# Program order from the first attention pair on, and weight steps moved from beside attention into the block products

## The chip, the cores and the metric

The kernel runs on one core of one Trainium2 chip, as one program. The metric is device time in microseconds (us) per execution. The kernel before took 1133.33 us, the median of three runs (1131.05 to 1134.03).

## The reference, cut to what matters

Chunked attention with a few memory keys feeds two dense layers in turn. Everything is fp32.

```python
batch, n_heads, seq, head_dim = (4, 8, 768, 64); n_mem = 8
chunk, left_ctx, right_ctx = (32, 16, 8)
for c in range(seq // chunk):                # each chunk of 32 queries sees at most 56 keys and 8 memory keys
    scores = scale * (q_c @ k_full.T)
    out[:, :, chunk_c] = softmax(scores) @ v_full
x = out.transpose(0, 2, 1, 3).reshape(3072, 512)
h = x @ w_in                                 # 512 -> 2048
x = np.maximum(0.01 * h, h) @ w_out          # 2048 -> 512
a, b = x @ w_a, x @ w_b                      # 512 -> 1536, twice
y = (a * b) @ w_out2                         # 1536 -> 512
```

## The kernel before

**Numbers.** TensorE works on fp32r operands. Each fp32 operand is split into a high part (a copy by ScalarE, ACT) and a low part (a subtraction by VectorE, DVE), and each product is three matmuls: low by high, high by low, high by high.

**Attention** is cut into 24 units of 128 tokens. A unit has 32 score matmuls (`a_scores`), a softmax on DVE and ACT, a transpose and 32 matmuls with the values. Units 0 to 7 are worked before or beside block 0 of the first dense layer; the other 16 go in pairs, and the list `STARTS` (18, 24, 29, ... 55, 60) says beside which item a pair begins.

**First dense layer, blocks 0 to 3.** The 3072 tokens are six blocks of 512. Blocks 0 to 3 are worked in items numbered 16 x block + f, with f one of 16 slices of the hidden width. One item has `mm1_pe` (12 matmuls into a PSUM tile `h`, of which there are two), `mm1_act` (ACT: the leaky relu, which releases `h`, and the copy `gh`; then DVE: the low part `gl`), and, two items late, `mm2` (12 matmuls into four PSUM tiles `a` that collect over all f). Block 0 has three more items (16 to 18 in its own counting), in which the second half of its tokens catches up on the first slices. When a block is done, ACT copies the four `a` tiles to SBUF tiles `x` (three buffers, tag `z`), and SyncE (SP) stores them to HBM. The next block's `mm2` needs the four `a` tiles free.

**Block products, blocks 4 and 5.** These two blocks are multiplied as 2 x 2 blocks with seven products in place of eight (the loop `for p in range(NF1 // 2)`, eight pairs of f slices). A pair has seven products of six matmuls (`prod`, into tiles A, B and C) and two `mm2`. The partial sums go through ACT snapshots `u` and DVE sums `s`; `relu` makes `g`, `gh` and `gl` of them, or, for block 5, a tile `g5` that is kept in SBUF. `late` is the last sum of a pair; its relu is written in the next pair. `s_sums` and `s_parts` make the summed weights (`zs`, `sc`, `sw`) for the pair to come.

**Weight steps.** The weights of the last two layers are split and combined ahead of time by the generator `prep_steps`, in 18 sets. `step()` takes two of its parts; four such steps (72 in all) make a set: two steps with a bias on ACT and a join on DVE for one 512 KB load `raw` each (tile `pz`), one step with copies on ACT (`pwa`) and four combinations and the low parts on DVE (`ps`, `pwa`), and one step with a copy on ACT and a low part on DVE (`pwb`) and the stores to HBM. In an item with n steps one part goes ahead of `mm1_pe`, and the other 2n - 1 stand between `mm1_pe` and `mm1_act`. The function `steps_at` says how many steps an item has.

**Order.** The framework's planner lists the instructions of each engine by its own estimate of when they are ready. `InOrder` replaces that by the order of the program for an engine while `on` is true. PE, DVE, ACT and SP are so from the start to the end of `first_items`; all four are then left to the planner for the rest of block 0, and PE, DVE and ACT are in program order again from item 16 (`if bi == 1 and f == 0`). In program order all instructions carry the line of the helper, L46 or L49. SBUF tiles of one tag take turns over a few buffers, so a writer can wait for the last reader of an older tile; tag `t` (tiles `g`, `u`, `sc`) has four.

**Last layers.** From about 613 us on the last two layers run, with TensorE busy almost without a gap.

Of the kernel before, what the change touches and what calls it, by code (L numbers as in the profile page):

```python
# [24 lines left out]
NF1, NF2 = F1 // P, F2 // P  # L25
# [30 lines left out]
def kernel(  # L56
# [68 lines left out]
    class Weights:  # L125
# [58 lines left out]
        def step(self):  # L184
            if self.joined < self.loaded:
                self.join()
                self.bias(self.joined + 2)
                self.low(self.joined - 1)
            else:
                self.low(self.joined)  # L190
# [218 lines left out]
    def x_raw():  # L409
        for h, tag in enumerate(("xh", "xl")):  # L410
            xr[NL + h] = xp.tile([P, KC, TB], F32, tag=tag, name="xr")
        for k in x4d:
            sp.dma_start(out=xr[NL][:, :, k * UT:k * UT + UT], in_=x4d[k])
# [10 lines left out]
    def x_tiles(key):  # L424
        hi = xp.tile([P, KC, TB], F32R, tag="xh", name="xh")
        lo = xp.tile([P, KC, TB], F32R, tag="xl", name="xl")
        x1[key] = (hi, lo)
# [87 lines left out]
    def mm1_pe(bi, parts):  # L515
        ps = ps_h.tile([P, TB], F32, tag="h", name="h")
        for o, n, f in parts:
            proj(ps, wslot[f, 0], x1["x", bi], slice(o, o + n))
        c = slice(min(o for o, _, _ in parts), max(o + n for o, n, _ in parts))
        return ps, c  # L520

    def mm1_act(ps, c, low=True):
        g = tp.tile([P, TB], F32, tag="t", name="g")
        act.activation(g[:, c], ps[:, c], AF.Prelu, alpha=0.01)
        gh = tp.tile([P, TB], F32R, tag="gh", name="gh", bufs=3)
        gl = tp.tile([P, TB], F32R, tag="gl", name="gl", bufs=3)
        act.copy(gh[:, c], g[:, c])

        def rest():
            dve.tensor_tensor(  # L530
                out=gl[:, c], in0=g[:, c], in1=gh[:, c].bitcast(F32), op=ALU.subtract
            )
            return gh, gl

        return rest() if low else rest

    def mm1(bi, parts):
        return mm1_act(*mm1_pe(bi, parts))
# [54 lines left out]
    def at(bi, f, fn, *args):  # L593
        beside.setdefault((bi, f), []).append(lambda: fn(*args))
# [78 lines left out]
    def at_item(i, *args):  # L673
        at(*divmod(i, NF1), *args)
# [20 lines left out]
    STARTS = (18, 24, 29, 34, 40, 45, 50, 55, 60)  # L695
# [191 lines left out]
    def wo_load(upto):  # L887
        while wo_next[0] < upto:
            b, f = 1 + wo_next[0] // NF1, wo_next[0] % NF1
            if b == NB3:  # L890
                break
            t = wop.tile([P, 2, 512], F32R, tag="wo", name="w")
            nc.sync.dma_start(out=t.bitcast(F32), in_=wod[f])
            wslot[f, 1] = t
            wo_next[0] += 1
# [21 lines left out]
    def y_part(i):  # L917
        t = y_raw(Y[i]).rearrange(two)
        hi, lo = [y_home(i, l) for l in range(2)]
        ya[i] = hi, lo  # L920
        hi, lo = hi.rearrange(two), lo.rearrange(two)
        act.copy(hi, t)
        dve.tensor_tensor(out=lo, in0=t, in1=hi.bitcast(F32), op=ALU.subtract)
# [21 lines left out]
        y_sub(1, 1, 2)  # L945

    def s_begin():
        s_sums(0)
        s_parts(0, 0)
        s_parts(0, 1)  # L950

# [2 lines left out]
    def s_sums(p):  # L954
        zs = []
        for f in (2 * p, 2 * p + 1):
            w = wslot[f, 0]
            z = tp.tile([P, 512], F32, tag="z", name="zs", bufs=3)
            dve.tensor_tensor(out=z, in0=w[:, 0].bitcast(F32), in1=w[:, 1].bitcast(F32), op=ALU.add)
            zs += [z[:, 0:256], z[:, 256:512]]  # L960
        z11, z12, z21, z22 = zs
        t = [tp.tile([P, 2, 256], F32, tag="t", name="sc") for _ in range(2)]
        for o, x, y, op in (
            (t[0][:, 1], z21, z22, ALU.add),
            (t[0][:, 0], t[0][:, 1], z11, ALU.subtract),
            (t[1][:, 0], z11, z21, ALU.subtract),
            (t[1][:, 1], z12, t[0][:, 0], ALU.subtract),
        ):
            dve.tensor_tensor(out=o, in0=x, in1=y, op=op)
        sums_[p] = t  # L970

    def s_parts(p, h):
        t = sums_[p][h]
        w = xa.tile([P, 2, 2, 256], F32R, tag="sw", name="sw", bufs=3)
        act.copy(w[:, 0], t)
        dve.tensor_tensor(out=w[:, 1], in0=t, in1=w[:, 0].bitcast(F32), op=ALU.subtract)
        for k, n in enumerate(((2, 3), (4, 6))[h]):
            sw[p, n] = w[:, :, k]
# [14 lines left out]

    at_item(max(STARTS), y_begin)
    at_item(max(STARTS) + 1, y_subs)
    at_item(max(STARTS) + 2, s_begin)

    def steps_at(i):
        if i < STARTS[0]:
            return 3  # L1000
        s = [x for x in STARTS if x <= i][-1]
        return (2, 1, 0, 0, 3, 2)[i - s] if s < STARTS[-1] else 0

    late = None
    for bi, f, parts in items[LEAD:]:
        i = (bi - 1) * NF1 + f
        first = bi == 0
        if f == 0 and not first:
            if bi + 1 < NL:
                x_tiles(("x", bi + 1))  # L1010
            else:
                x_raw()
        if bi == 1 and f == 0:
            for e in (pe, dve, act):
                e.on, e.last = True, None
        if first:
            W1.load(2 * f + 14)
            W1.step()
            behind.append((bi, parts, mm1(bi, parts)))
            W1.step()  # L1020
        else:
            n = steps_at(bi * NF1 + f)
            if n:
                next(steps, None)
            ps = mm1_pe(bi, parts)
            if late:
                behind.append(late[:2] + (late[2](),))
            for k in range(n):
                next(steps, None)
                if k + 1 < n:  # L1030
                    next(steps, None)
            late = bi, parts, mm1_act(*ps, low=False)
        if len(behind) >= LAG + first:
            mm2(*behind.pop(0))
        for fn in beside.get((bi, f), []):
            fn()
        if not first:
            wo_load(i + 3)
        elif f >= NF1 - 1:
            wo_load(f - NF1 + 2)  # L1040
            prep_load(f - NF1 + 1)
            if f > NF1:
                step()
    behind.append(late[:2] + (late[2](),))


    def relu(src, kept=None):
        g = tp.tile([P, TB], F32, tag="t", name="g")
        act.activation(g, src, AF.Prelu, alpha=0.01)
        if kept is None:  # L1050
            gh = tp.tile([P, TB], F32R, tag="gh", name="gh", bufs=3)
            gl = tp.tile([P, TB], F32R, tag="gl", name="gl", bufs=3)
        else:
            w = wp.tile([P, 2, TB], F32R, tag=f"wi{kept}", name="g5")
            gh, gl = w[:, 0], w[:, 1]
        act.copy(gh, g)

        def low():
            dve.tensor_tensor(out=gl, in0=g, in1=gh.bitcast(F32), op=ALU.subtract)
            return gh, gl  # L1060

        return low
# [26 lines left out]
    kept, late = {}, None  # L1089
    for p in range(NF1 // 2):  # L1090
        f0, f1 = 2 * p, 2 * p + 1
        A = ps_h.tile([P, TB], F32, tag="h", name="A")
        prod(A, p, 0, 0, True)
        Bk = ps_s.tile([P, TB], F32, tag="s", name="B")
        if not p:
            pe.matmul(Bk, wslot[0, 0][:, 0, 0:P], ya[0][0][:, 0], start=True, stop=True)
        act.copy(Bk, A)
        if p:
            low12 = relu(late, f1 - 2)
        else:  # L1100
            y_part(2)
        next2(behind.pop(0))
        if p:
            kept[f0 - 2] = low12()
        prod(Bk, p, 1, 1, False)
        g11 = relu(Bk)()
        if p + 1 < NF1 // 2:
            s_sums(p + 1)
        prod(A, p, 2, 4, False)
        u2 = snapped(A)  # L1110
        if p == 0:
            y_part(6)
        C = ps_s.tile([P, TB], F32, tag="s", name="C")
        prod(C, p, 3, 3, True)
        if p + 1 < NF1 // 2:
            s_parts(p + 1, 0)
            s_parts(p + 1, 1)
        prod(A, p, 4, 5, False)
        u3 = snapped(A)
        s22 = summed(u3, C)  # L1120
        next2(part2(NL, f0, g11))
        kept[f1] = relu(s22, f0)()
        if p:
            step()
        prod(A, p, 5, 2, False)
        low21 = relu(A)
        prod(C, p, 6, 6, False)
        behind.append(part2(NL, f1, low21()))
        if p:
            step()  # L1130
        late = summed(u2, C)
    low12 = relu(late, f1)
    next2(part2(NL + 1, 0, kept[0]))
# [518 lines left out]
```

## Time and profile before

| | |
|---|---|
| median of three runs | 1133.33 us |
| the profiled execution's own time | 1134.86 us |
| its span, first to last instruction | 1133.1 us |
| TensorE (PE) busy | 1101.9 us, 97% |
| VectorE (DVE) busy | 777.3 us, 69% |
| ScalarE (ACT) busy | 527.2 us, 47% |
| mean granted TensorE clock | 0.993 of full speed |

All times are us from the start of the span unless marked ns. A row of a timeline is one instruction, or several alike (x and their count); the bracket at its end is how long the engine was idle before it, and what ended that. The clock is the share of full speed that was granted; the two levels are 1.2 and 2.4 GHz. Stages: attention and block 0 up to about 129 us, blocks 1 to 3 beside attention to about 437, block products to about 565, the rest of block 5 to about 613, last layers to the end.

### The profile page before, as it was taken

Reading aid. Unit: us, or ns where it says so; the run is one execution under the profiler, and the core shown is the slowest. Engines: PE = TensorE matmul, PEld = TensorE weight load, DVE = VectorE, ACT = ScalarE, POOL = GpSimd, SP = SyncE. Lnnn points to the kernel's source line nnn. Section 1 sums busy time; section 2 is a strip of 40 time slices with the busy share of each in tenths; the row PEclk is TensorE's granted clock in tenths of the full one; section 3 lists DMA queues with packets and bytes.
Section 4 is the critical chain, followed back from the end, with each engine's and each line's share of the span. In section 5 each row is a group of like instructions: output and inputs, shape, how many; then the busy total and the mean of one; then the engine's idle time right before and its main releaser. Section 6 shows DMA issues by size and latency. Waiting matters only on the chain.

```text
span 1133.1 us, 16325 instructions
## 1 busy us (share of the span) xinstructions
PE 1101.9 (97%) x6195; PEld 914.1 (81%) x6195; DVE 777.3 (69%) x1417; ACT 527.2 (47%) x893; POOL 7.4 (1%) x18
## 2 busy tenths in 40 slices
PE   7899889999999999999999999999999999999997
PEld 6788768878888887877788888888888888888886
DVE  6796378989898877667540645678745678745666
ACT  5887454555555545565531434243433233343232
POOL 2000000000000000000000000000000000000000
PEclk9999979999999999999999999999999999999999
DMA  9996898889988862433586857576867476767452
GB/s 318 381 353 229 280 326 322 288 309 319 353 330 311 312 244 94 148 139 121 195 315 233 288 164 225 159 231 187 272 216 252 143 242 191 232 179 242 144 188 75
DMA packets 99855, 270.63 MB, mean 239 GB/s; under 512 B 9665, under 2 KB 24129, under 8 KB 99009
## 3 DMA queue, kind: packets, MB, share of 16 engines
q1 hardware_dynamic: 98032, 267.88, 69.5%
q10 hardware_dynamic: 1744, 1.70, 0.5%
q8 instruction: 49, 0.80, 0.3%
q14 instruction: 30, 0.24, 0.1%
HBM read 215.02 MB, written 54.53 MB: 238 GB/s over the span
## 4 chain that ended last, share of the span: by engine, by line
PE 85%; DVE 8%; ACT 3%; DMA 2%; issue 1%; SPq 0%; DVEq 0%; ACTq 0%
PE ca L49 18%; PE a L49 16%; PE cc L49 9%; PE oa L49 8%; PE h L49 8%; PE cb L49 5%; PE oy L49 4%; PE A L49 2%; PE pv L49 2%; DVE pt L49 2%; PE oz L49 1%; PE s L49 1%; PE h L432 1%; PE C L49 1%; PE h L433 1%; PE a L556 1%
## 5 line engine op out<-in xcount | busy, mean ns | idle before, releaser
L49 PE MATMUL ca<-ch,wab 128*128 128x512 f32 x576 | 192.5, 390 | 0.0
L49 PE MATMUL a<-gh,w 128*128 128x512 f32 (+1 forms) x536 | 175.6, 390 | 6.7 <-ACT x L49 6.2
L49 PE MATMUL h<-xh,w 128*128 128x512 f32 (+1 forms) x407 | 133.1, 390 | 4.3 <-ACT g L49 3.6
L49 ACT CAST st<-gb 128x512 fp32r<-128x512 f32 x126 | 76.5, 621 | 124.6 <-DVE gb L49 124.0
L49 PEld LDWEIGHTS ca<-ch,wab 128*128 128x128 f32 x576 | 108.2, 188 | 23.2 <-ACT a L49 0.5
L49 PEld LDWEIGHTS a<-gh,w 128*128 128x128 f32 x536 | 101.2, 190 | 29.1 <-ACT x L49 8.2
L49 PE MATMUL ca<-cl,wab 128*128 128x512 f32 x288 | 112.3, 390 | 0.0
L49 PE MATMUL a<-gl,w 128*128 128x512 f32 (+1 forms) x268 | 104.6, 390 | 3.0 <-DVE gl L49 3.0
L49 PE MATMUL oa<-st,wt 128*128 128x512 f32 x420 | 104.3, 389 | 0.0
L49 PE MATMUL cc<-ch,wab 128*128 128x512 f32 x288 | 100.5, 390 | 0.0
L49 DVE TENSOR_TENSOR st<-gb,st 128x512 fp32r<-128x512 f32 x126 | 85.3, 689 | 15.0 <-ACT st L49 13.3
L49 PEld LDWEIGHTS h<-xh,w 128*128 128x128 f32 x407 | 76.5, 190 | 20.3 <-ACT g L49 3.9
L49 PEld LDWEIGHTS oa<-st,wt 128*128 128x128 f32 x420 | 78.9, 188 | 16.3
L49 ACT COPY u<-ca 128x512 f32<-128x512 f32 x72 | 42.2, 586 | 91.6 <-PE ca L49 91.4
L49 DVE STREAM_TRANSPOSE pt<-p 32x128 f32<-32x128 f32 x256 | 77.4, 302 | 3.3
L49 PE MATMUL h<-xl,w 128*128 128x512 f32 (+1 forms) x204 | 78.9, 387 | 0.3 <-DVE xl L49 0.3
L49 PEld LDWEIGHTS cc<-ch,wab 128*128 128x128 f32 x288 | 54.1, 188 | 11.3
L49 PEld LDWEIGHTS ca<-cl,wab 128*128 128x128 f32 x288 | 54.1, 188 | 11.1
L49 PEld LDWEIGHTS a<-gl,w 128*128 128x128 f32 x268 | 51.0, 190 | 14.5 <-DVE gl L49 4.6
L49 DVE TENSOR_TENSOR gl<-g,gh 128x512 fp32r<-128x512 f32 (+1 forms) x67 | 45.2, 676 | 19.6 <-ACT gh L49 19.1
L49 PE MATMUL cc<-cl,wab 128*128 128x512 f32 x144 | 56.1, 390 | 0.0
L49 PE MATMUL oy<-st,wt 128*128 128x512 f32 x216 | 53.8, 389 | 0.0
(186 smaller groups left out, 1906.2 us busy)
## 6 DMA issues: line engine op xcount, KB each, us to landing
wab<-wab SPq DMA_DIRECT2D x126, 512.0 KB, 4.4
w<-wod SPq DMA_DIRECT2D x80, 512.0 KB, 5.5
raw<-w SPq DMA_DIRECT2D x68, 512.0 KB, 7.0
wt<-wtd SPq DMA_DIRECT2D x63, 512.0 KB, 4.4
k<-kl SPq DMA_DIRECT2D x48, 256.0 KB, 5.5
v<-vl SPq DMA_DIRECT2D x48, 256.0 KB, 5.8
wab<-pwb SPq DMA_DIRECT2D x12, 768.0 KB, 3.3
wod<-w SPq DMA_DIRECT2D x16, 512.0 KB, 6.4
```

Of the source, the lines that this page charges most:

```text
L49: self.last = emit(*args, **kwargs).ins
L432: pe.matmul(ps, w[1], x[0], start=first, stop=False)
L433: pe.matmul(ps, w[0], x[1], start=False, stop=False)
L556: pe.matmul(ps, slot[:, 1, c], gh[:, t], start=f == 0 and o == 0, stop=False, **kw)
```

## The change

The program order begins at item 18, where the first pair of units starts, instead of item 16. Items 16 and 17 have one step instead of three, the items 33 and 49 (the second item of a block) one instead of three, and the two steps at the end of block 0 are gone. The parts of the weights that are summed for the first pair of the block products (`s_parts`) are made one item later than `s_sums`. In the block products a pair has three steps in place of two, all behind the last sum of the pair before: at the start of the pair, behind the copy of A to B, and behind the first `mm2`; the low part of the late relu stands behind the one of product 1.

```diff
     def s_begin():
-        s_sums(0)
         s_parts(0, 0)
         s_parts(0, 1)
...
-    at_item(max(STARTS) + 2, s_begin)
+    at_item(max(STARTS) + 2, lambda: s_sums(0))
+    at_item(max(STARTS) + 3, s_begin)
 
     def steps_at(i):
-        if i < STARTS[0]:
-            return 3
-        s = [x for x in STARTS if x <= i][-1]
+        s = max((x for x in STARTS if x <= i), default=None)
+        if s is None or i % NF1 == 1:
+            return 1
         return (2, 1, 0, 0, 3, 2)[i - s] if s < STARTS[-1] else 0
...
-        if bi == 1 and f == 0:
+        if bi * NF1 + f == STARTS[0]:
             for e in (pe, dve, act):
                 e.on, e.last = True, None
...
             prep_load(f - NF1 + 1)
-            if f > NF1:
-                step()
...
     for p in range(NF1 // 2):
         f0, f1 = 2 * p, 2 * p + 1
+        if p:
+            step()
         A = ps_h.tile([P, TB], F32, tag="h", name="A")
         prod(A, p, 0, 0, True)
...
         act.copy(Bk, A)
         if p:
+            step()
             low12 = relu(late, f1 - 2)
         else:
             y_part(2)
         next2(behind.pop(0))
         if p:
-            kept[f0 - 2] = low12()
+            step()
         prod(Bk, p, 1, 1, False)
         g11 = relu(Bk)()
+        if p:
+            kept[f0 - 2] = low12()
         if p + 1 < NF1 // 2:
             s_sums(p + 1)
...
         kept[f1] = relu(s22, f0)()
-        if p:
-            step()
         prod(A, p, 5, 2, False)
         low21 = relu(A)
         prod(C, p, 6, 6, False)
         behind.append(part2(NL, f1, low21()))
-        if p:
-            step()
         late = summed(u2, C)
```

## Rows read from the trace of the kernel before

**Rows 1.** Waits of PE, two stretches: total us, times, longest us

```profile
PE a L49 <- ACT x L49: 1.9, 2, 1.0
...
PE a L49 <- DVE gl L49: 3.0, 4, 0.9
```

**Rows 2.** One window: busy PE, PEld, DVE, ACT, POOL; clock, DMA share, GB/s

```profile
145.60:155.70 10.10, 5.78 (x12) 3.68 (x12) 3.90 (x7) 4.95 (x10) 0.00 (x0) 0.60 0.97 365
```

**Rows 3.** Timeline of PE behind item 17: start us, us, instruction, idle before

```profile
141.25 0.80 PE L49 MATMUL h<-xh,w 128*128 128x512 f32 x1 [3.65 <-ACT g L49]
...
148.33 0.80 PE L49 MATMUL a<-gh,w 128*128 128x512 f32 x1 [2.73 <-ACT x L49]
...
154.13 0.79 PE L49 MATMUL a<-gh,w 128*128 128x512 f32 x1 [1.59 <-ACT x L49]
```

**Rows 4.** Timeline of ACT in the same stretch

```profile
135.50 0.67 ACT L106 ACTIVATE raw<-raw 128x512 f32<-128x512 f32 x1 [4.10 <-DMA raw<-w]
...
139.10 1.04 ACT L49 CAST pwb<-ps 128x1024 fp32r<-128x1024 f32 x1 [1.31 <-DVE ps L49]
...
140.62 0.57 ACT L49 ACTIVATE g<-h 128x512 f32<-128x512 f32 x1
...
153.70 0.37 ACT L49 COPY x<-a 128x256 f32<-128x256 f32 x1 [4.88 <-DMA x2d<-x]
```

**Rows 5.** Chain that ended last, 120 to 195 us: start us, us, what

```profile
128.51 6.97 DMA raw<-w
...
149.05 4.55 DMA x2d<-x
...
155.77 2.94 PE s L49 x64
...
164.38 2.72 PE h L49 x12
...
193.59 1.87 PE s L49 x64
```

**Rows 6.** Timeline of ACT in item 33

```profile
249.76 1.05 ACT L49 CAST pwb<-ps 128x1024 fp32r<-128x1024 f32 x1 [1.18 <-DVE ps L49]
```

**Rows 7.** Groups of the steps' instructions, 456 to 565 us: busy us, mean ns

```profile
L49 DVE SCALAR_TENSOR_TENSOR pz<-raw,pz 128x512 int32<-128x512 int32 x6 | 4.2, 693 | 0.2
...
L49 ACT ACTIVATE raw<-raw 128x512 f32<-128x512 f32 x6 | 4.1, 679 | 0.0
...
L49 DVE TENSOR_TENSOR pwb<-ps,pwb 128x1024 fp32r<-128x1024 f32 x3 | 3.7, 1219 | 0.0
...
L49 ACT CAST pwb<-ps 128x1024 fp32r<-128x1024 f32 x3 | 3.2, 1050 | 0.7 <-DVE ps L49 0.7
...
L49 DVE TENSOR_TENSOR pwa<-pz,pwa 128x256 fp32r<-128x256 f32 (+1 forms) x7 | 3.1, 495 | 0.0
...
L49 ACT CAST pwa<-pz 128x256 fp32r<-128x256 f32 (+1 forms) x7 | 2.9, 463 | 0.0
...
L49 DVE TENSOR_SCALAR pz<-raw 128x512 int32<-128x512 int32 x6 | 2.5, 421 | 0.0
...
L49 DVE TENSOR_TENSOR ps<-pz 128x256 f32<-128x256 f32 x6 | 2.5, 418 | 0.0
```

**Rows 8.** Timeline of PE: end of attention, and second pair of the block products

```profile
437.80 0.50 PE L49 MATMUL a<-gl,w 128*128 128x512 f32 x1 [0.37 <-DVE gl L49]
...
488.48 0.50 PE L49 MATMUL a<-gl,w 128*128 128x512 f32 x1 [0.83 <-DVE gl L49]
```

**Rows 9.** Timeline of ACT and DVE ahead of the second of these waits

```profile
486.05 0.62 ACT L49 CAST gh<-g 128x512 fp32r<-128x512 f32 x1
...
487.74 0.68 DVE L49 TENSOR_TENSOR gl<-g,gh 128x512 fp32r<-128x512 f32 x1
```

**Rows 10.** Timeline of ACT and PE in the first pair, which has no step

```profile
448.36 0.59 ACT L49 COPY u<-A 128x512 f32<-128x512 f32 x1 [0.81 <-DVE gl L49]
...
449.00 1.67 PE L49 MATMUL A<-y,sw 128*128 128x512 f32 x6
```

## The prediction

> **What bounds the kernel now.** I read the page first: TensorE (PE) is busy for 97% of the span, so a change can only pay where PE waits or runs slowly. The waits of PE come next, then the windows to see where the clock falls, then the timelines at those places, and last the chain, for what the waiting hangs on. The largest loss is behind item 17. PE stops three times, for 3.65, 2.73 and 1.59 us [rows 3], and the granted clock, 0.99 over the span, is 0.60 there, between its levels of 2.4 and 1.2 GHz [rows 2]. The reader is to see in ACT's timeline why: ACT waits 4.10 us for the load `raw` of a step, does the step's copies (`pwb` at 139.10, behind DVE's combinations), and only at 140.62 the leaky relu of item 16, which releases the tile `h` that PE waits for [rows 4]. The third wait is for the fourth copy `x`, which waited 4.88 us for a store of `x2d` to free its buffer [rows 4]; that store was issued at 149.05 and took 4.55 [rows 5]. Beyond that there are two waits at the ends of blocks 1 and 2, 1.9 us together, and four for `gl` around the block products, 3.0 us together [rows 1]. Everywhere else that the change touches, PE runs without a wait.
>
> **Items 16 and 17.** PE went idle at 137.60 (141.25 less 3.65) [rows 3] and finished the scores of the first pair at 158.71 (155.77 and 2.94) [rows 5]: 21.1 us. The work in it is item 18's `mm1`, an `mm2` of twelve and 64 score matmuls, 2.72, 2.72 and 1.87 at full clock [rows 5], so 7.3. The loss is 13.8 us, stops and slow clock together; that is the most that can come back.
> What could stay: the planner may still put the bias of the second `raw`, which lands at 135.48 (128.51 and 6.97) [rows 5], and the first copies of item 18's step ahead of the relus of 16 and 17, since these need no PE. The copies end at about 138.3: the bias ends at 136.2 [rows 4], a join is 0.69 and 0.42, copies 0.97 (2.9 over three sets) [rows 7]. The next cast (`pwb`) can't come ahead: DVE's combinations stand behind item 17's `gl` in program order. So `h` comes free at 138.9 instead of 141.2, PE waits about 1.3; the four copies `x` begin at about 140.7, and with a store as slow as the 4.55 seen the fourth ends at 146.1, which PE needs at 143.8: a wait of 2.3. That bad list gives back 13.8 - 3.6 = 10.2, a list without it 13.8. I take 11.5, nearer to the bad one, because a list by estimated readiness favours what needs no PE. The far ends are 0 (the same list as now, by program order, [rows 4]) and a loss of one more wait as long as the 4.10 for `raw`.
> The Trainium skill (DMA: Bandwidth & Descriptors, Anatomy of one DMA) fits a transfer as 2.0 us and its bytes at 436 GB/s, for the GpSimd path; for this 128 KB store that is an estimated 2.3 us. The trace had 4.55 for it on SP's queue [rows 5]. By the skill's figure the last wait would nearly vanish and this term be about 13; I keep the row.
> The steps that leave this stretch, six with the two at the end of block 0, take their loads and stores along, out of a window with DMA share 0.97 [rows 2]. That can only help `k`, `v` and `w` behind them on SP's queue.
>
> **Items 33 and 49.** There the copies `x` that free the four `a` tiles stand on ACT behind three steps and a relu; the step's cast at 249.76 waited 1.18 for DVE [rows 6], and PE waited for the copies, 1.9 in two places [rows 1]. With one step the relu can start when item 33's `mm1` ends and the copies when their `mm2` ends; no wait is left. The first matmul behind such a wait takes 0.50 [rows 8], some 0.1 over the others, so I count 2.0 (bounds 0 and 2.1). Elsewhere the items keep their steps, only which of the four kinds falls on which item changes by two; both arrangements occur already without a wait.
>
> **End of attention.** `s_parts` one item later stands behind `gl` of item 62 instead of ahead of it, and the wait of 0.37 [rows 8] goes: 0.45 with the restart.
>
> **Block products.** Before, a step with combinations stood between the last two relus of every second pair. In the second pair `gh` was ready at 486.67 and `gl` began at 487.74, behind them [rows 9]; PE waited 0.83 [rows 8]. Of the 3.0 [rows 1], 2.6 is of this kind, at three pairs; with restarts 2.95 goes.
> New is a third step per pair, 21 where there were 12, and one at the end where nothing waits. By [rows 7] a set of four is 6.15 us on DVE and 3.4 on ACT, so 1.54 and 0.84 a step. A pair is 66 matmuls, 14.96 us at 2.72 per twelve [rows 5]. I count from its first product. The copy of A to B is due at 4.08, the snapshot `u` behind product 2 at 8.16, `gl` of the last relu at 1.59 of the next pair. Product 1 ends at 5.6 and its relu, copy and `gl` need 2.0, so `gl` ends at 7.6. The low part of the late relu, now behind it, is 0.6 on DVE, and pushes sums, `sw`, the next sum, both relus, so that the last `gl` ends at 1.4 of the next pair: 0.2 before it is due. The late sum then ends at 2.0, and the three steps begin. In the worst order (join, combine, cast) a join takes 1.1, copies 1.0, the late relu 1.25 on ACT, the `pwb` cast 1.05: product 1's relu starts at 6.25, 0.6 late, and the next pair's last `gl` 0.45 late. By counting steps (50 before the first pair) the orders are bad in pairs 2, 5 and 6 of seven and harmless in the others: 3 x 0.45 = 1.4, and I take 1.5. The lower bound is 0. The upper is a buffer: `u` has tag `t` with four buffers, and in the first pair, where there is no late relu, it waited 0.81 for `gl` to free one, which cost PE 0.19 at 449.00 [rows 10]. If in the other pairs it gets the late relu's buffer, freed only behind the moved low part, it ends 1.35 late: seven times, 9.5. I hold that unlikely, since the tiles `sc` and `u` take buffers in the order in which these come free, and older ones are free by then.
> On SP the added loads `raw` stand among the loads `w`, which are issued four `mm2` ahead, two pairs or 30 us; the slowest raw took 6.97 [rows 5]. No cost.
>
> **Sum.** 11.5 + 2.0 + 0.45 + 2.95 - 1.5 = 15.4. The profiled execution took 1134.86, so 1119.5 for it; it lies 1.5 above the median of 1133.33, so 1118 as a median.
>
> **Rivals**, as medians.
> (a) All of it comes back: 13.8 + 2.0 + 0.45 + 2.95 = 19.2, less nothing, so 1114. For it: block 0 up to 129 us, which the planner lists, shows no such wait in the last 70 us. Against: the raw load that is late by 4.10 stays late.
> (b) The planner's list keeps half of the stop, and the clock falls in it. The wait of 1.3 for `h`, one near the 2.73 of [rows 3], the scores at 2.94 instead of 1.87 and one `mm2` at double length (2.72 more) are 7.8, which leaves 6 of the first term: 1123 to 1124. The Trainium skill (TensorE: Matmul & The Clock Gate, HAM oscillation) says that gaps without matmuls drop the array to half clock. The trace agrees behind the wait of 3.65, with 0.60 granted [rows 2].
> (c) The buffer of the late relu: 9.5 in place of 1.5, so 1126. It decides from `u` on: a copy `u` that waits for `g5`'s low part.
> (d) The stop stays whole, since the list comes out as program order gave it: the rest is 3.9, so 1129 to 1132.
> (e) Slower: the steps between a pair's last sum and product 1's relu form a closed chain with the sums behind it. If nothing of the third step (1.54 and 0.84) and of the moved low part (0.69) finds cover, each of seven pairs is 3.1 longer: 22 in place of 1.5, so 1138. It turns the sum from 2.4 a pair on. For it: the chain has little slack (0.2 by my count). Against: DVE and ACT have idle stretches in a pair for most of what is added.
>
> **Chances.** Forecast (1116 to 1121.5) 0.54, (a) 0.16, (b) 0.16, (c) 0.05, (d) 0.04, (e) 0.05. The range of 1113 to 1125 holds the forecast, (a) and (b), about 0.85. About 0.3%, 3.4 us, is what a measurement can tell from no change: faster 0.91, the same 0.04 (case (d), which lies at that bound), slower 0.05 (case (e)).
>
> **What would show it.** Right: between 130 and 146 PE waits less than 4 us together and the clock stays at 1.00; the first pair's scores come 11 to 13 us sooner; no wait for `x` at the ends of blocks 1 and 2; none for `gl` in the middle of a pair with a step of combinations, and at most three of 0.5 at starts of pairs. Wrong: relus of items 16 and 17 behind a cast `pwb` on ACT; `u` waiting for a low part in every pair; pairs longer than 15.5 us.

## The result, and the profile after

The changed kernel took 1117.99 us, median of four runs (1116.82 to 1118.13), against 1133.26 (1131.05 to 1134.03, four runs by now) for the kernel before: a ratio of 0.9866, 95% interval 0.9849 to 0.9883. The forecast was 1118, in a range of 1113 to 1125.

The waits of PE come first, from 120 to 600 us of the kernel after: total us, times, longest us.

```profile
PE a L49 <- ACT x L49: 0.6, 1, 0.6
PE A L49 <- ACT u L49: 0.4, 1, 0.4
```

The two waits for `x` at the ends of blocks 1 and 2 and the four for `gl` [rows 1] are gone; a wait for a snapshot `u` is new. Next the windows of the kernel after: length, busy PE, PEld (TensorE's weight loads), DVE, ACT and POOL with their counts, granted clock, DMA share, GB/s.

```profile
125.00:135.00 10.00, 10.00 (x88) 9.00 (x88) 2.93 (x5) 6.13 (x10) 0.00 (x0) 1.00 0.80 243
135.00:145.00 10.00, 9.42 (x76) 7.62 (x76) 5.41 (x10) 5.33 (x11) 0.00 (x0) 1.00 0.75 294
```

Where PE was busy for 5.78 of 10.10 us at a clock of 0.60 [rows 2], it now runs at 1.00, with 0.58 us of idle time in 20. Three marks of PE's timeline in the kernel after cut the span into stages: the values of the last unit beside block 0 (`pv`), the scores of the first pair (`s`), and the first product of the last layers (`ca`); the row with the wait for `x` stands between.

```profile
125.14 1.15 PE L385 MATMUL pv<-pt,v 128*64 128x64 f32 x32
126.23 0.39 PE L46 MATMUL h<-xh,w 128*128 128x256 f32 x1
...
137.56 0.40 PE L46 MATMUL h<-xh,w 128*128 128x512 f32 x1
...
143.10 0.50 PE L49 MATMUL a<-gh,w 128*128 128x512 f32 x1 [0.58 <-ACT x L49]
...
144.00 2.08 PE L49 MATMUL s<-k,qz 128*64 128x64 f32 x64
...
593.68 0.39 PE L49 MATMUL ca<-ch,wab 128*128 128x512 f32 x1
```

With the first pair product A (at 440.43 before, 424.65 after) the stages are as follows, in us, each kernel by its own timeline of PE; the kernels below the first two are those of the experiments, described there.

| kernel | front: `pv` to the end of the scores | attention: to the first A | blocks: to the first `ca` | rest | span |
|---|---|---|---|---|---|
| before | 33.69 | 281.72 | 170.00 | 522.67 | 1133.1 |
| after | 20.94 | 278.57 | 169.03 | 522.62 | 1116.3 |
| order16 | 20.07 | 278.57 | 168.91 | 523.01 | 1115.4 |
| order18 | 20.06 | 278.57 | 169.02 | 522.80 | 1115.9 |
| order_alone | 34.71 | 281.92 | 170.03 | 522.72 | 1133.4 |
| pairs_before | 20.06 | 278.57 | 172.78 | 522.58 | 1117.9 |
| steps16 | 25.11 | 281.80 | 170.60 | 522.24 | 1123.9 |
| six | 20.06 | 279.59 | 171.02 | 522.38 | 1117.1 |
| steps33 | 20.63 | 278.88 | 169.01 | 522.62 | 1115.1 |
| sparts_together | 21.07 | 279.28 | 168.95 | 522.60 | 1115.8 |
| low_back | 20.93 | 278.58 | 167.39 | 522.53 | 1113.5 |
| best_low | 20.06 | 278.58 | 167.33 | 522.56 | 1112.6 |

After against before: 12.75 in the front, 3.15 in attention, 0.97 in the blocks, 16.9 together; the spans differ by 16.8. The medians differ by only 15.3, since the profiled execution of before (1134.86) lies 1.5 above its median and that of after (1118.13) 0.1 above. The start up to `pv` differs by up to 1.6 us between these kernels; read the stages, not the spans.

**One point told wrongly ahead of the prediction.** The new condition, `bi * NF1 + f == STARTS[0]`, holds twice: for item 18 of block 1 (bi 1, f 2) and before that for the last added item of block 0 (bi 0, f 18). The two L46 rows above show it, for L46 is the first instruction of an order. The order so begins one item *earlier* than before, at 126.23, and is taken up anew at 137.56. The prediction had items 16 and 17 left to the planner; they are not. ACT's timeline of the kernel after shows that stretch.

```profile
132.15 0.60 ACT L49 ACTIVATE g<-h 128x512 f32<-128x512 f32 x1
...
135.53 0.66 ACT L49 ACTIVATE raw<-raw 128x512 f32<-128x512 f32 x1 [2.12 <-DMA raw<-w]
137.41 0.40 ACT L49 CAST pwa<-pz 128x256 fp32r<-128x256 f32 x1 [1.22 <-DVE pz L49]
137.72 0.59 ACT L49 ACTIVATE g<-h 128x512 f32<-128x512 f32 x1
...
138.87 0.92 ACT L49 COPY x<-a 128x256 f32<-128x256 f32 x3
141.24 1.05 ACT L49 CAST pwb<-ps 128x1024 fp32r<-128x1024 f32 x1 [1.45 <-DVE ps L49]
142.19 0.59 ACT L49 ACTIVATE g<-h 128x512 f32<-128x512 f32 x1
142.68 0.36 ACT L49 COPY x<-a 128x256 f32<-128x256 f32 x1
```

Before, the relu of item 16 stood behind the late load, two casts and a second bias and began at 140.62 [rows 4]. Now it begins at 132.15, ahead of the wait for `raw`, which is still 2.12 us. Behind that wait stand a cast `pwa`, the relu of item 17, three copies `x`, a cast `pwb`, one more relu and the fourth copy `x`, all later by it, and this copy is late by 0.58 for PE.

### The profile page after: what moved, and what is told of

It reads as the page before. It is cut to its first block, busy times and chain, and to the rows that moved or that the text cites. A ratio compares the mean times of both kernels' runs of the same rounds, so it can differ in the third digit from the quotient of the medians.

```text
span 1116.3 us, 16345 instructions
## 1 busy us (share of the span) xinstructions
PE 1096.2 (98%) x6195; PEld 909.6 (81%) x6195; DVE 777.8 (70%) x1417; ACT 526.9 (47%) x893; POOL 7.4 (1%) x18
## 4 chain that ended last, share of the span: by engine, by line
PE 92%; DVE 3%; ACT 3%; DMA 1%; issue 1%; SPq 0%; DVEq 0%; ACTq 0%
PE a L49 19%; PE ca L49 18%; PE h L49 11%; PE cc L49 9%; PE oa L49 8%; PE cb L49 5%; PE oy L49 4%; PE A L49 3%; PE s L49 2%; PE pv L49 2%; PE oz L49 1%; PE h L432 1%; PE C L49 1%; PE h L433 1%; PE a L556 1%; PE h L434 1%
## 5 line engine op out<-in xcount | busy, mean ns | idle before, releaser
L49 ACT ACTIVATE g<-h 128x512 f32<-128x512 f32 (+1 forms) x51 | 29.8, 585 | 60.9 <-PE h L49 60.8
```

The lines of the kernel that those rows point to most:

```text
L49: self.last = emit(*args, **kwargs).ins
```

## The experiments

The theory was A: the fewer steps beside attention bring the gain, and where the program order begins brings none. Its rival B: the order brings it. Beside that, each later term was taken alone. Ratios are to runs of the kernel before that were made beside each kernel: a median of 1134.37 for order16, order18, order_alone and pairs_before, 1133.99 for low_back, t5, steps33 and sparts_together, 1134.94 for steps16, six, no_lead and best_low.

### Where the order begins

order16 is the kernel after, order_alone the kernel before, each with the other's condition; order18 is the kernel after with the order from item 18 alone.

```diff
-        if bi * NF1 + f == STARTS[0]:
+        if bi == 1 and f == 0:          # order16
+        if bi == 1 and f == 2:          # order18
```

> The changed kernel with one line put back: program order begins at item 16 of block 1, as before the change. In the changed kernel the condition (block x 16 + f equal to 18) is true twice, first for the last item of block 0, so its order begins one item earlier than before and is taken up anew at item 18. Theory A, that the fewer steps in items 16 and 17 bring the gain of 12.6 us there: scores of the first pair still end at 146 to 147, time 1117 to 1119. Theory B, that the place where the order begins or is taken up anew brings it: scores end at 150 to 158, time 1122 to 1130.

> The changed kernel with the order beginning only at item 18, so that items 16 and 17 and the end of block 0 are listed by the planner: what the prediction took the change to be. Theory A (fewer steps): scores of the first pair end within 2 us of 146.1, time 1116 to 1120. The prediction's bad list (bias and first copies ahead of both relus, fourth copy of x late): scores end at 148 to 149, time 1120 to 1121. Theory B (order): more than 1122.

> The kernel before with only the condition of the change: order from the last item of block 0, taken up anew at item 18; three steps in items 16 and 17 and the two at the end of block 0 as before. Theory A: no gain, 1131 to 1136, the same three waits of PE behind item 17. Theory B: 1121 to 1126.

Measured: order16 1117.20 us, ratio 0.9851 (0.9837 to 0.9866); order18 1117.57, 0.9855 (0.9840 to 0.9869); order_alone 1134.88, 1.0003 (0.9993 to 1.0012). B falls: the new condition alone gives nothing, and PE still waits 3.91 for the relu of item 16 there. Neither order16 nor order18 has the wait for `x`; their fronts are 0.9 shorter than the kernel after's. That is the price of the order's place at most: of the kernels with the new condition and few steps, the front is 20.06 in one and 20.6 to 21.1 in four. What sets these apart is the late load. The one is pairs_before, whose front is that of the kernel after line for line; its `raw` was there without a listed wait. ACT's bias in pairs_before, then bias and relu of item 17 in order16:

```profile
132.27 0.68 ACT L49 ACTIVATE raw<-raw 128x512 f32<-128x512 f32 x1
...
135.62 0.68 ACT L49 ACTIVATE raw<-raw 128x512 f32<-128x512 f32 x1 [2.51 <-DMA raw<-w]
136.18 0.60 ACT L49 ACTIVATE g<-h 128x512 f32<-128x512 f32 x1
```

With the new condition, PE's wait for the fourth `x` grows with ACT's wait for `raw`: 0.27 at 1.81 (steps33), 0.58 at 2.12 (the kernel after and low_back), 0.72 at 2.25 (sparts_together). In order16 ACT waits 2.51 and PE not at all, since the relu stands directly behind the bias and no cast of a step ahead of the copies. So the new place of the order costs only where this load is late; why it is late in one execution and not in the next, these traces don't show.

### Steps of items 16 and 17, and at the end of block 0

Both kernels are the kernel before; steps16 has the first edit, six both.

```diff
         if i < STARTS[0]:
-            return 3
+            return 1
...
-            if f > NF1:
-                step()
```

> The kernel before, with one step each in items 16 and 17 instead of three, and nothing else: four steps fewer, one whole set, so every later item gets the kind of step that it had. Theory A (the steps of items 16 and 17 alone make the stop): PE's waits of 3.65 and 2.73 us go and the clock stays at 1.00; 10 to 12.6 us less, 1121 to 1124. Rival B (the program order that starts earlier, or the two steps at the end of block 0, carry a good part): under 8 us less, 1126 or more. On the waits for x at the ends of blocks 1 and 2: theory N (three steps in one item are too many there) and theory K (the kind of step that falls on these items decides) both expect them here again, 1.9 together, since neither number nor kind is changed.

> The kernel before, with one step each in items 16 and 17 and without the two steps at the end of block 0: six steps fewer, a set and a half, so every later item gets the kind of step two further back. Items 33 and 49 keep three steps. Theory K (the kind of step that falls on the last items of blocks 1 and 2 decides): the waits of PE for x there, 1.9 before, are under 0.3. Theory N (their number decides): they stay at 1.9. On items 16 and 17 as in the kernel with four steps fewer, so the time is 1120 to 1123 by K and 2 more by N.

Measured: steps16 1125.63 us, ratio 0.9921 (0.9900 to 0.9942); six 1119.43, 0.9865 (0.9851 to 0.9880). Six steps fewer make the whole of the front's gain, 13.63 us; four of them only 8.58, less than theory A had said for them, and a long wait and a fall of the clock, which A had gone, are still there. The two at the end of block 0 are worth the other 5.05. The timelines of SP and ACT in steps16 show how (SP's rows are issues of DMAs).

```profile
137.81 0.33 SPq L810 DMA_DIRECT2D wab<-pwa  x1
138.23 0.38 SPq L811 DMA_DIRECT2D wab<-pwa  x1
139.88 0.32 SPq L819 DMA_DIRECT2D wab<-pwb  x1
140.25 0.42 SPq L820 DMA_DIRECT2D wab<-pwb  x1
140.77 2.39 SPq L575 DMA_DIRECT2D x2d<-x  x3
...
139.38 0.92 ACT L49 COPY x<-a 128x256 f32<-128x256 f32 x3
144.39 0.37 ACT L49 COPY x<-a 128x256 f32<-128x256 f32 x1 [4.10 <-DMA x2d<-x]
...
144.82 0.50 PE L49 MATMUL a<-gh,w 128*128 128x512 f32 x1 [2.67 <-ACT x L49]
145.71 3.55 PE L49 MATMUL s<-k,qz 128*64 128x64 f32 x64
```

The same in six:

```profile
136.40 0.92 ACT L49 COPY x<-a 128x256 f32<-128x256 f32 x3
138.83 0.37 ACT L49 COPY x<-a 128x256 f32<-128x256 f32 x1 [1.52 <-DMA x2d<-x]
...
136.79 1.30 SPq L575 DMA_DIRECT2D x2d<-x  x3
...
142.03 2.08 PE L49 MATMUL s<-k,qz 128*64 128x64 f32 x64
```

In steps16 a set ends just there. Its four stores of weights stand ahead of the stores of `x` on SP's queue; the first `x2d` is issued 1.39 us after its copy began, against 0.39 in six, and takes 3.52 to land by the chain of waits. The fourth `x` waits 4.10, PE 2.67, and the scores behind that wait run at the lower clock (3.55 for the same 64 matmuls that took 2.08; the window from 145 to 155 has 0.83 granted). In six the set has not come so far; the stores are issued at once. That is read from the timelines: no run takes away two steps and leaves the part of the set that falls here. The fit of the Trainium skill (DMA: Bandwidth & Descriptors, Anatomy of one DMA), which is for the GpSimd path, gives an estimated 2.3 us for such a store; of the eight `x2d` stores from 120 to 150 us of steps16 the first three take 1.9, the other five 2.7 to 3.7, so the fit is near the first ones and not the one that decided.

### Items 33 and 49

steps33 is the kernel after with three steps in these two items again.

```diff
-        if s is None or i % NF1 == 1:
+        if s is None:
```

> The kernel after, with three steps again in items 33 and 49, the last items of blocks 1 and 2 (by counting, the other items keep their number, so four steps fewer are left for later). My term: two waits of PE for the copies x return, of about 0.9 each, and the first pair product A comes 2.0 us later, the time is 1120. Rival: the copies wait for nothing, since the steps of these items are by now other ones of the four kinds and their casts are ready, and PE waits less than 0.5 in both places together; the time is 1118 to 1118.5.

(They are the second items of blocks 2 and 3, in which the last `mm2` of blocks 1 and 2 is worked.)

Measured: 1116.94 us, ratio 0.9852 (0.9835 to 0.9868), 1.05 below the kernel after, of another group of runs, and so below the rival's range too. By the waits the rival holds: PE has none for `x` in these places, and attention takes 278.88 against 278.57, 0.3 more where my term said 2.0. With steps16 and six the cause is settled. The waits of PE in steps16, 120 to 600 us:

```profile
PE a L49 <- ACT x L49: 4.8, 4, 2.7
```

It has two of before's waits there (0.91 at 242.98 and 0.96 at 343.61), and attention takes 281.80 as before. six, with the same three steps in items 33 and 49, has none, and takes 279.59. Four steps fewer are one whole set and change nothing in what later items get; six are a set and a half, and shift it by two kinds. So it is the kind of step that falls on these items, not the number of steps: before it was the part whose cast `pwb` waited 1.18 for DVE directly ahead of the relu and the copies [rows 6]. In six the copies come directly behind the relu, and that cast behind them:

```profile
232.63 2.15 ACT L49 COPY x<-a 128x512 f32<-128x512 f32 x4
...
238.78 1.05 ACT L49 CAST pwb<-ps 128x1024 fp32r<-128x1024 f32 x1 [1.70 <-DVE pwa L49]
```

### End of attention

sparts_together is the kernel after with `s_parts` at the item of `s_sums` again.

```diff
-    at_item(max(STARTS) + 3, s_begin)
+    at_item(max(STARTS) + 2, s_begin)
```

> The kernel after, with s_parts back beside s_sums at the end of attention (both at item 62). My term: the wait of PE of 0.37 there returns, and the time is 0.45 more, 1118.4. Rival: the wait belonged to the steps that stood there and not to s_parts, and the time is the same within 0.2.

Measured: 1117.66 us, ratio 0.9857 (0.9840 to 0.9874). The total can't tell it (0.3 below the kernel after, of another group of runs), the stage can: the wait of 0.4 for `gl` is back, and attention takes 279.28, 0.71 more.

### The block products

pairs_before is the kernel after with the whole loop over pairs as before; eight steps are left for the end of the loop. low_back puts one line back.

```diff
         next2(behind.pop(0))
         if p:
             step()
+            kept[f0 - 2] = low12()
         prod(Bk, p, 1, 1, False)
         g11 = relu(Bk)()
-        if p:
-            kept[f0 - 2] = low12()
```

> The changed kernel with the loop over pairs as before (two steps per pair at their old places, the late low part ahead of product 1; eight steps are left over and run behind the last pair). Theory by the traces: pairs cost 3.4 us of waits instead of 2.5, so 0.9 slower than the changed kernel, three waits for gl of 0.8 to 0.9 back, no wait of u for gl except in the first pair. Theory by the prediction: 1.45 slower. Rival: the eight steps left over delay the last layers' operands, and it is 2 us or more slower, with a wait at about 575 to 600.

> The kernel after, with one line of a pair put back: the low part of the late relu stands ahead of product 1 again, behind the pair's third step. In the kernel after seven pairs take 15.28 to 15.68 us where 14.96 is the length without a wait, 2.54 together, and in each the copy u on ACT waits for the gl of product 1's relu. Theory U (u takes the buffer that product 1's relu holds, and the place of the low part decides which buffer that is): u waits for nothing of DVE in most pairs, the pairs come to about 15.0, and the time is 1.5 to 2.5 us less, 1115.5 to 1116.5. Rival V (DVE and ACT simply have too much to do ahead of product 2 with a third step): the low part ahead of product 1 delays product 1's gl by its own 0.6, the pairs grow by 0.3 to 0.6 each, and the time is 2 to 4 us more, 1120 to 1122.

Measured: pairs_before 1120.44 us, ratio 0.9885 (0.9868 to 0.9902); low_back 1115.47, 0.9838 (0.9818 to 0.9858). In pairs_before the three waits for `gl` are back (2.6), and the eight steps left over cost more behind the loop, as its rival had it (2.45 slower; PE waits 1.4 for a load `w` at 576), so its 3.75 us in the blocks are not the loop's worth alone. From the first copy of A to B to the last, its seven pairs take 108.51 against 107.60, the 0.9 of the theory by the traces. low_back takes 167.39 in the blocks where the kernel after takes 169.03. The kernel after, ACT and DVE and PE in its third pair, and the first and last copy of A to B:

```profile
461.50 0.60 ACT L49 ACTIVATE g<-B 128x512 f32<-128x512 f32 x1 [0.35 <-PE B L49]
...
463.56 0.59 ACT L49 COPY u<-A 128x512 f32<-128x512 f32 x1 [0.81 <-DVE gl L49]
...
462.78 0.69 DVE L49 TENSOR_TENSOR gl<-g,gh 128x512 fp32r<-128x512 f32 x1 [0.38 <-ACT gh L49]
463.39 0.69 DVE L49 TENSOR_TENSOR g<-g,g 128x512 fp32r<-128x512 f32 x1
...
464.20 1.23 PEld L49 LDWEIGHTS A<-y,sw 128*128 128x128 f32 x6 [0.44 <-ACT u L49]
...
426.44 0.57 ACT L49 COPY B<-A 128x512 f32<-128x512 f32 x1 [2.84 <-PE B L49]
...
534.04 0.57 ACT L49 COPY B<-A 128x512 f32<-128x512 f32 x1 [0.75 <-PE A L49]
```

The same in low_back, in its fourth pair:

```profile
475.33 0.60 ACT L49 ACTIVATE g<-B 128x512 f32<-128x512 f32 x1 [0.83 <-PE B L49]
...
476.75 0.59 ACT L49 COPY u<-A 128x512 f32<-128x512 f32 x1 [0.17 <-DVE g L49]
...
475.98 0.68 DVE L49 TENSOR_TENSOR g<-g,g 128x512 fp32r<-128x512 f32 x1
476.61 0.69 DVE L49 TENSOR_TENSOR gl<-g,gh 128x512 fp32r<-128x512 f32 x1
...
425.37 0.57 ACT L49 COPY B<-A 128x512 f32<-128x512 f32 x1 [2.84 <-PE B L49]
...
531.33 0.57 ACT L49 COPY B<-A 128x512 f32<-128x512 f32 x1 [0.88 <-PE A L49]
```

In the kernel after the low part of the late relu (DVE `g` at 463.39) stands behind product 1's `gl`. The snapshot `u` then begins at the end of that `gl` (462.78 and 0.69 is 463.47): it has the buffer of product 1's relu. PE's next weights wait 0.44 for it. In low_back the low part comes first, `u` begins 0.09 after it ends, ahead of the end of `gl`, and the weights don't wait. The listed wait of PE is short, since most of it lies with the weight load; the length of the pairs has it all. From the first copy B to the last, seven pairs take 107.60 us in the kernel after and 105.96 in low_back; seven without a wait would be 104.72 (7 x 14.96). The kernel after so loses 2.88; the 2.54 of the expectations leaves out the first pair. By the time theory U holds (1115.47, at the edge of its 1115.5 to 1116.5; V had 1120 to 1122), and four of the seven pairs take 14.96. It said too much for `u`: in five pairs of low_back `u` waits for the late relu's low part instead, 0.17 to 0.74, and the second pair still takes 15.64.

### A fifth buffer, and where the weights lie

t5 is the kernel after with five buffers of tag `t` in the room of two unused tiles; no_lead only loses one of these tiles.

```diff
-    lead = ctx.enter_context(tc.tile_pool(name="lead", bufs=1, side="left"))   # t5, no_lead
-    lead.tile([P, 224], F32, tag="lead", name="lead")                          # t5, no_lead
-    sm.tile([P, 344], F32, tag="pad", name="pad", bufs=1)                      # t5
-    tp = ctx.enter_context(tc.tile_pool(name="tp", bufs=4, side="right"))      # t5
+    tp = ctx.enter_context(tc.tile_pool(name="tp", bufs=5, side="right"))      # t5
```

> The kernel after, with a fifth buffer for the tiles of tag t (g, u, pwa and their like), in room that two unused tiles held; no instruction is added or moved by hand. Theory U (the 2.54 us that seven pairs lose are the wait of u for a buffer that product 1's relu holds): u takes an older buffer, no wait of u for gl is left, the pairs come to about 15.0 and the time is 1115.3 to 1116.7. Rival V (too much work on DVE ahead of product 2): g is no earlier, PE waits for the same sums, the pairs stay at 15.3 to 15.7 and the time at 1117.5 to 1118.5. Elsewhere a fifth buffer can change the listed order of block 0 by some tenths in either direction.

> The kernel after without the unused tile lead of 896 bytes, which is the first on the left side of SBUF: every tile of that side lies 896 bytes lower, the right side (t, z, the small tiles) stays, and there are four t buffers as before. In the kernel with five t buffers the 128x512 matmuls with weights from w, wab and wt took 392 to 396 ns instead of 389, those with weights from sw 389, and the time was 23 us more. Theory P (the address of the weights on the left side decides): the matmuls are 395 ns again, all but those with sw, and the time is 1138 to 1142. Rival R (the fifth buffer or the right side's addresses did it): the matmuls are 389 ns and the time is 1117 to 1119.

Measured: t5 1140.83 us, ratio 1.0064 (1.0047 to 1.0082); no_lead 1139.42, 1.0041 (1.0026 to 1.0056). Neither theory of t5 had 23 us more. The wait that it was made for is gone: no `u` waits for `gl`, and most pairs take 15.28 us, against 15.54 to 15.63 in no_lead with its four buffers; seven pairs take 107.50 against 108.94 (the `sw` matmuls of t5 are a little shorter too). So a buffer more does nearly what the other place of the low part does, which bears theory U out a second time. The time went into the matmuls themselves. Groups of instructions by form, in the kernel after (count, busy us, mean ns):

```profile
L49 PE MATMUL ca<-ch,wab 128*128 128x512 f32 x576 | 192.2, 389 | 0.0
L49 PE MATMUL oa<-st,wt 128*128 128x512 f32 x420 | 104.3, 389 | 0.0
L49 PE MATMUL C<-y,sw 128*128 128x512 f32 x96 | 24.3, 389 | 0.0
```

and in no_lead:

```profile
L49 PE MATMUL ca<-ch,wab 128*128 128x512 f32 x576 | 195.6, 395 | 0.0
L49 PE MATMUL oa<-st,wt 128*128 128x512 f32 x420 | 105.9, 392 | 0.0
L49 PE MATMUL C<-y,sw 128*128 128x512 f32 x96 | 24.6, 392 | 0.0
```

Theory P holds for the time: with the left side of SBUF 896 bytes lower and nothing else changed, nearly all 128x512 matmuls take 391 to 397 ns instead of 389, at the same granted clock (0.999). It misses on `sw`, which was to stay at 389.

### Both gains together

best_low is low_back with order16's condition.

> The kernel after, with program order from the first item of block 1 as in the kernel before, and the low part of the late relu ahead of product 1 again. If the two gains add up, 0.6 to 0.9 from the order and 1.6 to 2.5 from the low part, the time is 1114.6 to 1115.8 and the first pair's scores come 20 us behind the pv matmul instead of 20.9. Rival: the order's gain was scatter between executions, and the time is that of the low part alone, within 0.3 of 1115.5.

Measured: 1114.91 us (1114.43 to 1115.92), ratio 0.9826 (0.9811 to 0.9840). It beats both kernels. Its front takes 20.06 as forecast and its blocks 167.33, so by the stages the gains add up; by the medians its 0.56 us over low_back are inside the scatter.

## Why the prediction came out right, step by step

**Items 16 and 17: mechanism right, list wrong, sum 1.25 low.** The stop and the slow clock were indeed the steps' doing, and 13.63 was there to be had (33.69 less 20.06), close to the 13.8 that I worked out. But the bias did not come "ahead of the relus of 16 and 17", by either order. In program order with one step an item the relu of item 16 stands ahead of the load that is late, so 12.75 came back and not 11.5. The misread condition doesn't excuse the list: in order18, where the planner has items 16 and 17 as I took it, the relu of item 16 begins at 132.46, the bias at 133.80, and the front is 20.06. The wait for the fourth `x` was put at 2.3, by a store of 4.55, and is 0.58: the store (issued at 139.26) took 1.9, and the copy stood behind the late load and the casts. The estimate of about 13 that I set aside for that row was the nearer one.

**The two steps at the end of block 0 were not priced.** I let their DMAs only help the loads behind them. By the timelines they decide which part of a set meets the copies `x`: without their removal the wait for `x` is 2.67 (I had 2.3 for it with them removed), and the front 5.05 longer.

**Items 33 and 49: size right (2.0 against 2.2 between steps16 and six), cause wrong.** I gave it to the smaller number of steps, and said of the shift of kinds that "both arrangements occur already without a wait". The shift alone does it; the smaller number alone is worth 0.3.

**End of attention:** 0.45 against 0.71, the mechanism as described. The stage adds up from the runs: 2.2 for the kinds, 0.7 for `s_parts`, 0.3 for the number, where 3.15 came.

**Block products: what went is right but was sized too low, what came is another wait.** The three waits for `gl` are gone. I counted 0.83 for one and a restart, as the matmuls list it; the weight load in front of it had waited 1.26, and the two pairs around it lost 1.13 (31.05 us from copy to copy of A to B, against 29.92). In the kernel before, PEld and ACT:

```profile
488.48 0.19 PEld L49 LDWEIGHTS a<-gl,w 128*128 128x128 f32 x1 [1.26 <-DVE gl L49]
...
472.50 0.57 ACT L49 COPY B<-A 128x512 f32<-128x512 f32 x1 [0.47 <-PE A L49]
...
503.55 0.57 ACT L49 COPY B<-A 128x512 f32<-128x512 f32 x1 [0.46 <-PE A L49]
```

So three such waits were worth about 3.5, and not 2.95 (an estimate: 1.13 and 1.15 for two, and 1.2 for the third, which ends behind the last copy). The new cost was put at 1.5, from a last `gl` 0.45 late in pairs 2, 5 and 6. No such wait is there. The stage gave 0.97, so the cost was about 2.5, or 2.0 by my 2.95; the pairs agree (2.88, of which the first pair had lost 0.36 before too). low_back, at 167.39, takes 1.64 of it away with the place of one DVE instruction. The failed step is "older ones are free by then": `u` gets a buffer that has just been used, that of product 1's relu, freed by the `gl` just ahead, and not the late relu's. The 9.5 of rival (c) has the right tag and, for the kernel after, the wrong tile; in low_back, where the low part comes first, it is that tile, at a much smaller price.

**Sum.** 15.4 was forecast for the profiled executions, and 16.8 came, 1.4 more. I also took off 1.5 to come to a median, as before's profiled execution lies that far above its own; after's lies only 0.1 above. The two errors cancel, so 1118 met 1118 partly by luck: the terms were off by +1.25, +0.7 and -0.5.

**Rivals.** (a) would have had all 13.8; the front came to 0.88 of it, and order16 has it all. (b), (d) and (e) did not occur: the clock is 1.00, and a pair takes 15.3 to 15.7 where (e) had 18. The longest pair, 15.68, is over the 15.5 that I named as a sign against me; PE waits for `u` in it. The signs for me came: between 130 and 146 us PE waits 0.58, the clock is 1.00, and the first pair's scores end 12.6 sooner.

## What to carry to other kernels

When side work is spread over items in a fixed cycle, taking away steps also changes which kind meets each tight place; count modulo the cycle, and look which kinds stand ahead of the copies and stores that free the bottleneck's buffers. An instruction that nobody waits for can still set which buffer the next tile gets: here the place of one low part was worth 1.6 us. And evaluate a new condition for every index that reaches it, not only for the one that it is meant for.

## What was not expected of the hardware

The address of tiles in SBUF moved the duration of matmuls at an unchanged granted clock: 896 bytes less ahead of the left side turned 389 ns into 391 to 397 and cost some 21 us (1139.42 against 1117.99). Weight loads stayed at 187 to 189 ns in no_lead and in t5, which has the same shift. Whether the weights' or the moving operand's address decides, and by what mechanism, stays open.
